# Seven half-size products for the first feed-forward product of two token blocks

## The chip, the cores and the metric

One core of a Trainium2 chip runs the kernel. The metric is the device time of one execution in microseconds (us); lower is better. Each kernel is run several times and the median is given.

## What is computed

A sparse attention over 8 batches, 8 heads and 576 positions is followed by a feed-forward layer over its 4608 x 512 output:

```python
attn = softmax(where(mask, scale * q @ k.T, -1e9))      # heads 0-3: last 32 positions
x = (attn @ v).transpose(0, 2, 1, 3).reshape(4608, 512) # heads 4-7: every 32nd position
h = x @ w_in                                            # 512 x 2048
r = maximum(h, 0)
g = s * (r * r) + b
out = g @ w_out                                         # 2048 x 512
```

The change concerns only `h`, `r` and their squares, for the last 1024 of the 4608 tokens.

## The kernel before

The 4608 tokens are cut into 9 blocks (T = 0 to 8) of 512 tokens. The transposed attention output lies in four tiles `xT` (128 of the 512 features each) that hold three batches of 576 tokens at a time. For each block there is a first product (`ff1`, line 912): for each of 16 groups of 128 hidden features (`ft`), four matmuls of 128 x 128 weights by 512 tokens add up in one bank of PSUM (line 922, 64 matmuls a block). ScalarE takes the bank out with a relu into `u` (line 948), VectorE in a few places (line 950). Two groups at a time are squared into `gT`, on VectorE (line 958) or ScalarE (line 956).

The second product of blocks 0 and 1 is a plain one (`ff2`, line 970). From block 2 on it is `ff2_seven` (line 792): the 512 tokens and 512 output columns are halved, and a Strassen scheme of seven products takes the place of eight quarter products. It needs sums of quarters of `gT` (`sums_post`, line 743, VectorE, line 759), sums of `w_out` formed once (`mix_post`, line 773), 112 matmuls of 256 columns a block (line 890), and evictions that add an earlier result (lines 809, 821 and 832, VectorE). The output goes out by DMA from SyncE's queue.

The order of all instructions comes from a planner (`class Plan`, line 16) that runs while the program is built. It keeps a modelled time, with a cost for each step. TensorE's steps are emitted one by one into a single queue: attention steps, first-product steps and second-product steps. A first-product step goes when what it needs is modelled as done; at every fourth step the second product goes first if the first is more than one block ahead (the main loop at the end of the kernel). Work for the other engines is posted with its needs and a cost for each engine that may take it (`post`, line 41, and `flush`, line 44), and the engine that would be done first gets it. `LATER` lets squares and sums (`g`, `S`) stand back by 1.5 us. PSUM has eight banks in groups `t` (1), `s` (2), `a` (1), `f1` (2) and `f2` (2); a `Group` of matmuls takes the bank of its list that comes free first. On the chip each engine works its queue in order and waits at semaphores.

The last attention steps are issued at about 216 us. After that TensorE has only the two products.

Of the kernel before, what the change touches and what calls it, by code (L numbers as in the profile page):

```python
# [8 lines left out]

FP16 = mybir.dt.float16  # L10
FP32 = mybir.dt.float32
# [4 lines left out]
class Plan:  # L16
# [7 lines left out]
    LAT = {"A": 70.0, "V": 70.0, "P": 70.0, "D": 12000.0, "X": 7000.0, "Y": 12000.0}  # L24

    SLACK = 800.0
    LATER = {"g": 1500.0, "S": 1500.0, "in": 2500.0, "w_mix": 2500.0}

    def __init__(self):
        self.t = 0.0  # L30
# [93 lines left out]
def kernel(  # L124
# [11 lines left out]
    nc = tc.nc  # L136
# [64 lines left out]
    v_str = [const.tile([SQ, 4, ST, D + 1], FP16, name=f"v_str{i}") for i in range(NV)]  # L201
# [16 lines left out]
    p_taken = {True: 0, False: 0}  # L218

    SR = 80  # L220
    ks = [const.tile([SR, 4 * ST * D], FP16, name=f"ks{i}") for i in range(2)]

# [190 lines left out]
    def bank(group):  # L413
        return ps[group.name]
# [310 lines left out]

    SQ_ACT = 0
    SEVEN = 2
    H = NFT // 2

    def ff_order(T):  # L730
        if T < SEVEN:
            return list(range(NFT))
        return [f + g for f in (0, 4) for g in (0, 1, 2, 3, 8, 9, 10, 11)]
# [6 lines left out]
    def roomy(T):  # L740
        return T >= NBLK - 2

    def sums_post(T):

        at2, at4 = ("S2", "S4") if roomy(T) else ((0, 0), (0, 1))
        for h in range(2):
            fs = slice(4 * h, 4 * h + 4)

            def make(out, x, y, op, fs=fs):
                def at(w):  # L750
                    if w in own:
                        if (w, T) not in gts:
                            gts[w, T] = (sp if w == "S" else inp).tile(
                                [128, H, 256], FP16, tag=own[w], name="S")
                        return gts[w, T][:, fs]
                    return part_of(T, *w, fs)

                def g(eng):
                    nc.vector.tensor_tensor(out=at(out), in0=at(x), in1=at(y), op=op)  # L759
# [3 lines left out]
            ns = {"V": 690.0}  # L763
# [28 lines left out]
    def ff2_seven(T):  # L792
# [119 lines left out]
    def ff1(T, ft, ct, group, cts=(0, 1, 2, 3), early=False):  # L912
        tok0 = T * PS
        def f():
            if ft == 0 and ct == cts[0]:
                gts[T] = gp.tile([128, NFT, PS], FP16, tag="gT", name="gT")
            if ct == cts[0]:
                gts["h", T, ft] = bank(group)
            at = tok0 % (NX * S)
            n = min(PS, NX * S - at)  # L920
            for lo, hi in ((0, n), (n, PS))[:1 + (n < PS)]:
                nc.tensor.matmul(  # L922
                    out=gts["h", T, ft][:, lo:hi],
                    lhsT=w_in_sb[ft // 4][:, ct].rearrange("p (x l) -> p l x", l=4)[:, ft % 4],
                    rhs=xT[ct][:, (at + lo) % (NX * S):(at + lo) % (NX * S) + hi - lo],
                    start=(ct == cts[0] and lo == 0), stop=(ct == cts[-1] and hi == PS))

        needs = [("xT", bb, c) for bb in {tok0 // S, (tok0 + PS - 1) // S}
                 for c in ((ct,) if early else range(4))]
        needs.append(("w_in", ft // 4))  # L930
        if ft == 0 and ct == cts[0] and T >= 2:
            needs.append(("F2", T - 2))
        s = Step(f, 216, needs=needs, group=group if ct == cts[0] else None)
        if ft == 0 and ct == cts[0] and T >= SEVEN:
            s.after = lambda: sums_post(T)
        if ct == cts[-1]:
            key = ("h", T, ft)
            s.keys = [key] + ([("F1", T)] if ft == NFT - 1 else [])
# [29 lines left out]
        return s  # L968

    def ff2(T, ts, ft, group, part=0, parts=1):  # L970

# [198 lines left out]
    for T in range(NBLK):  # L1170
        if T == 0:

            gr = [Group("s", SB, "f1", F1B) for _ in range(4)]
            cts = FIRST
            f1 += [ff1(T, ft, ct, gr[ft], cts, True) for ct in cts for ft in range(4)]
        for ft in ff_order(T)[0 if T else 4:]:
            gr = Group("f1", F1B, "f2", F2B) if T == 0 else Group("f1", F1B)
            for ct in range(4):
                f1.append(ff1(T, ft, ct, gr))
        if T == 0:  # L1180

# [12 lines left out]
        if T >= SEVEN:  # L1194
            f2 += ff2_seven(T)
            continue
        for ts in range(4):

            parts = 2 if T == NBLK - 1 and ts == 3 else 1
            for part in range(parts):  # L1200
                gr = Group("f2", F2B)
                for ft in range(NFT):
                    f2.append(ff2(T, ts, ft, gr, part, parts))
                    f2[-1].pos = T + 0.25 + (ts + (part + ft / NFT) / parts) / 4
    plan.t = 1850.0

    def keep_running(until):
# [24 lines left out]

    def due():

        pos = i1 / 64.0 + (f2[i2 - 1].pos if i2 else 0.0) + 0.1
        return (pos if pos <= 1 else 1 + (pos - 1) / 2) * batch_ns

    while i2 < len(f2) or any(at_i[p] < len(att[p]) for p in range(len(att))):
# [14 lines left out]
            order.append(1)  # L1253
        if i2 < len(f2):
            order.append(2)
        if len(order) == 2 and i1 % 4 == 0 and i1 / 64.0 > (f2[i2 - 1].pos if i2 else 0.0) + 1:
            order.reverse()
        if i1 % 4:
            order = [1]
# [53 lines left out]
```

The softmax here doesn't subtract the row's maximum and nothing guards it: scores larger than these inputs give would overflow.

## Time and profile before

| what | value |
|---|---|
| median of 3 runs | 303.96 us (303.76 to 304.38) |
| span of the profiled execution, first to last instruction | 300.1 us |
| difference of the median and that span | 3.86 us |
| TensorE busy | 292.4 us |
| VectorE busy | 220.2 us |
| ScalarE busy | 182.1 us |
| GpSimd busy | 93.0 us |
| granted TensorE clock, mean | 0.998 |

The profiled execution has no separate total: its span runs from its first to its last instruction, and what a run's time has besides is given here as the difference of the median and that span. In a profile, PE is TensorE, PEld its weight loads (which run beside the matmuls), DVE VectorE, ACT ScalarE, POOL GpSimd, SP SyncE. L922 is line 922. The chain of waits is followed back from the last instruction to whatever released it. A row of a group of instructions gives line, engine, operation, output and inputs, shape and count, then busy us and mean ns of one, then the engine's idle time before them and what ended it. Ends of matmuls are modelled, and neighbours overlap, so the distance of their starts says more than their durations.

### The profile page before, as it was taken

What the parts mean: (1) busy time and instruction counts of PE and PEld (TensorE: products, weight loads), DVE (VectorE), ACT (ScalarE), POOL (GpSimd) and SP (SyncE); (2) the same over time, 40 slices, a digit from 0 to 9 for tenths busy, and PEclk for the clock granted to TensorE, in tenths of its full rate; (3) what the DMA queues carried; (4) which work ended last, traced back from release to release, by engine and by line L of the source; (5) the groups of instructions that cost most, each with busy time, mean ns of one, the idle gap of its engine ahead of it and who ended that gap; (6) DMA issues with size and microseconds to landing.
All of it is one profiled execution on the core that took longest, in us unless ns stands there. A gap on an engine that the chain in (4) does not pass through costs nothing.

```text
span 300.1 us, 6846 instructions
## 1 busy us (share of the span) xinstructions
PE 292.4 (97%) x2704; PEld 209.3 (70%) x2704; DVE 220.2 (73%) x462; ACT 182.1 (61%) x326; POOL 93.0 (31%) x140
## 2 busy tenths in 40 slices
PE   7899989999999999999999999999999999999995
PEld 3775655666556558889766876688888577766884
DVE  6857797779876788687877897689766366647663
ACT  3577966889547788638774976488535545444300
POOL 8873442700950495008720494300000000000000
PEclk9999999999999999999999999999999999999999
DMA  8999999999999499999999999996141110200213
GB/s 136 178 204 201 169 214 185 202 163 157 100 189 160 67 128 130 152 181 128 150 137 178 149 170 131 135 154 167 40 96 38 69 35 2 105 0 2 94 66 123
DMA packets 106434, 38.17 MB, mean 127 GB/s; under 512 B 85698, under 2 KB 104258, under 8 KB 106402
## 3 DMA queue, kind: packets, MB, share of 16 engines
q0 software_dynamic: 60848, 18.23, 64.3%
q1 hardware_dynamic: 45554, 19.51, 36.7%
q8 instruction: 21, 0.34, 0.5%
q14 instruction: 11, 0.09, 0.1%
HBM read 36.99 MB, written 10.62 MB: 159 GB/s over the span
## 4 chain that ended last, share of the span: by engine, by line
PE 85%; DMA 9%; POOL 3%; issue 1%; ACT 0%; DVE 0%; POOLq 0%
PE ps_f L922 37%; PE ps_f L890 25%; PE ps_f L979 8%; PE ps_s L565 4%; DMA kl<-in_k_dram 4%; DMA w_out_sb<-in_moe_w_out_dram 3%; PE ps_a L626 2%; DMA vs<-in_v_dram 2%; PE ps_s L890 2%; PE ps_t L626 1%; PE ps_t L890 1%; PE ps_s L979 1%; PE ps_t L444 1%; POOL v_str L346 1%; PE ps_t L673 1%; PE ps_a L890 1%
## 5 line engine op out<-in xcount | busy, mean ns | idle before, releaser
L922 PE MATMUL ps_f<-xT,w_in_sb 128*128 128x512 f16 (+4 forms) x696 | 147.3, 340 | 0.0
L948 ACT ACTIVATE u<-ps_f 128x512 f16<-128x512 f32 x139 | 81.9, 595 | 67.0 <-PE ps_f L922 66.5
L922 PEld LDWEIGHTS <-w_in_sb 128*128 128x128 f16 x704 | 71.7, 113 | 30.6 <-issue 0.3
L890 PEld LDWEIGHTS <-gT 128*128 128x128 f16 x608 | 58.4, 98 | 13.6
L890 PE MATMUL ps_f<-w_out_sb,gT 128*128 128x256 f16 x376 | 53.7, 273 | 0.0
L958 DVE TENSOR_TENSOR gT<-u 128x1024 f16<-128x1024 f16 x48 | 32.8, 684 | 15.0 <-ACT u L948 14.2
L979 PE MATMUL ps_f<-w_out_sb,gT 128*128 128x512 f16 x112 | 29.4, 379 | 0.8 <-DMA w_out_sb<-in_moe_w_out_dram 0.8
L583 ACT ACTIVATE p_str<-ps_s 72x432 f16<-72x432 f32 (+1 forms) x45 | 20.4, 483 | 9.7 <-PE ps_s L565 9.2
L956 ACT ACTIVATE gT<-u 128x1024 f16<-128x1024 f16 x24 | 25.4, 1057 | 0.7
L653 DVE TENSOR_TENSOR x_nat<-ps_a,rec 96x384 f16<-96x384 f32 (+2 forms) x46 | 23.9, 519 | 0.7
L583 ACT ACTIVATE p_loc<-ps_s 128x384 f16<-128x384 f32 x46 | 21.4, 495 | 4.7 <-PE ps_s L565 4.2
L759 DVE TENSOR_TENSOR gT<-gT 128x1024 f16<-128x1024 f16 x34 | 22.5, 682 | 2.1 <-ACT gT L956 1.9
L890 PE MATMUL ps_f<-w_mix,gT 128*128 128x256 f16 x176 | 23.8, 273 | 0.0
L890 PEld LDWEIGHTS <-S 128*128 128x128 f16 x176 | 17.1, 98 | 4.4
L324 POOL DMA_DIRECT2D v_loc<-in_v_dram x24 | 17.8, 766 | 6.9 <-PE ps_f L626 3.8
L979 PEld LDWEIGHTS <-gT 128*128 128x128 f16 x128 | 11.5, 98 | 10.5 <-DMA w_out_sb<-in_moe_w_out_dram 1.2
L329 POOL DMA_DIRECT2D v_str<-in_v_dram x16 | 13.0, 817 | 13.0 <-PE ps_f L890 2.8
L626 PEld LDWEIGHTS <-p_str 72*128 72x128 f16 x256 | 13.2, 98 | 5.4
L1050 POOL COPY gate<-kT 1x1 f16<-1x1 f16 x6 | 2.9, 490 | 45.2 <-DMA kT<-ks 45.1
L643 DVE RECIPROCAL rec<-ps_a 96x6 f32<-96x6 f32 (+2 forms) x46 | 8.4, 183 | 11.3 <-PE ps_a L626 11.1
L890 PE MATMUL ps_f<-w_mix,S 128*128 128x256 f16 x112 | 15.7, 273 | 0.0
L759 DVE TENSOR_TENSOR S<-gT 128x1024 f16<-128x1024 f16 x18 | 11.8, 684 | 0.1
(163 smaller groups left out, 407.3 us busy)
## 6 DMA issues: line engine op xcount, KB each, us to landing
out_dram<-o SPq DMA_DIRECT2D x34, 256.0 KB, 2.4
w_in_sb<-in_moe_w_in_dram POOLq DMA_DIRECT2D x4, 512.0 KB, 10.4
w_out_sb<-in_moe_w_out_dram POOLq DMA_DIRECT2D x4, 512.0 KB, 11.7
qs<-in_q_dram POOLq DMA_DIRECT2D x6, 288.0 KB, 7.3
ks<-in_k_dram POOLq DMA_DIRECT2D x6, 288.0 KB, 9.5
v_loc<-in_v_dram POOLq DMA_DIRECT2D x24, 72.0 KB, 10.0
ql<-in_q_dram POOLq DMA_DIRECT2D x4, 288.0 KB, 9.3
kl<-in_k_dram POOLq DMA_DIRECT2D x16, 72.0 KB, 4.0
```

Of the source, the lines that this page charges most:

```text
L324: nc.gpsimd.dma_start(out=vl[LPAD:128, h, :, 0:D], in_=v_band(b, h))
L329: nc.gpsimd.dma_start(out=vs[:, h, :, 0:D], in_=v[b, 4 + h].rearrange("(p j) d -> p j d", j=ST))
L583: nc.scalar.activation(out=st["pw", g][0:nk, 0:2 * n * nq], in_=st["s", g][0:nk, 0:2 * n * nq], func=AF.Exp, scale=scale)
L626: nc.tensor.matmul(out=st["pa", g][:, n % 6, :], lhsT=st["pw", gp_][0:nk, i * nq:i * nq + WIDE], rhs=vt[0:nk, 2 * mm + e, j, :])
L653: nc.vector.tensor_tensor(out=x_at(0, cnt), in0=st["pa", g][0:nq, 0:cnt, 0:D], in1=st["rec", g][0:nq, 0:cnt].to_broadcast([nq, cnt, D]), o ...
L759: nc.vector.tensor_tensor(out=at(out), in0=at(x), in1=at(y), op=op)
L890: nc.tensor.matmul(out=gts[name, T, t][:, 0] if halves else gts[name, T][:, t], lhsT=lhs(k, t), rhs=rhs(k), start=fresh and k == 0 and (ha ...
L922: nc.tensor.matmul(out=gts["h", T, ft][:, lo:hi], lhsT=w_in_sb[ft // 4][:, ct].rearrange("p (x l) -> p l x", l=4)[:, ft % 4], rhs=xT[ct][: ...
L948: nc.scalar.activation(out=u, in_=gts["h", T, ft], func=AF.Relu)
L956: nc.scalar.activation(out=g, in_=u, func=AF.Square)
L958: nc.vector.tensor_tensor(out=g, in0=u, in1=u, op=ALU.mult)
L979: nc.tensor.matmul(out=gts[id_], lhsT=gts[T][:, ft, ts * 128:(ts + 1) * 128], rhs=w_out_sb[:, ft, cols], start=(ft == 0), stop=(ft == NFT ...
```

## The change

Blocks 7 and 8 (`FIRST7 = NBLK - 2`) no longer go through `ff1`. `ff1_seven` cuts the hidden features (2 x 1024), the input features (2 x 256) and the tokens (2 x 256) in halves and uses the Strassen scheme with seven products. A block has four units of 2 x 256 hidden features; a unit has seven products of four 256-column matmuls each (2 groups of 128 hidden features by 2 of 128 input features), 112 matmuls a block.

- P1, P6, P5 and P3 of a unit add up in one bank, "A". After P1, P6 and P5 its content is copied to an f32 tile (V1, U, E), and the next product waits for that copy. After P3 the bank itself is one quarter of `h`, and a relu takes it out.
- P2 has a bank "C" of its own and is added to V1. P7 has a bank "D" and is added to E; then P4 adds to D, which is added to U.
- The three additions are VectorE's `TENSOR_ADD_SAT`, max(min(a + b, 3e38), 0): the relu is inside the addition. The relu of P3 and the copies may go to ScalarE or VectorE, as may the squares, two per unit.
- `combine_w` forms four sums of quarters of `w_in` on VectorE (eight instructions of 1024 columns) once, after the last attention products. They lie in tiles that the attention had used (`ks`, `v_str`), which grow to 128 partitions.
- `combine_x` forms four differences of quarters of `xT` per block (eight instructions of 256 columns, VectorE), in `qD_loc` for block 7 and `p_loc` for block 8.
- For the last block the second product's order becomes P1, P7, P6, P5, P2, P4, P3 (before, P6 came ahead of P7).
- The main loop's count of first-product steps is 112 for these blocks in place of 64 (`f1_pos`).

```diff
+    FIRST7 = NBLK - 2
+    SUM_P = None
...
-        seq = [seq[i] for i in ((0, 3, 4, 1, 2, 5, 6) if roomy(T) else (0, 2, 3, 4, 1, 5, 6))]
+        seq = [seq[i] for i in ((0, 4, 3, 1, 2, 5, 6) if last else (0, 3, 4, 1, 2, 5, 6) if roomy(T) else (0, 2, 3, 4, 1, 5, 6))]
...
+    def combine_w():
+
+        def w(h, j, i):
+            return w_in_sb[2 * h + i][:, 2 * j:2 * j + 2]
+
+        B1, B2 = B - 2, B - 1
+        AFTER = [("a", (B2, m), 1) for m in range(4)]
...
+        for i in range(2):
+            for n, x, y, op, more in (
+                    (1, w(1, 0, i), w(1, 1, i), ALU.add, []),
+                    (2, w_sum[1][:, i], w(0, 0, i), ALU.subtract, [("wc", 1, i + 1)]),
+                    (3, w(0, 0, i), w(1, 0, i), ALU.subtract, []),
+                    (4, w(0, 1, i), w_sum[2][:, i], ALU.subtract, [("wc", 2, i + 1)])):
+                plan.post(AFTER + held[n] + more, {"V": 690.0},
...
+    def combine_x(T):
...
+            for n, x, y, needs in (
+                    (1, x_part(T, 0, 1, c), x_part(T, 0, 0, c), lo + held),
+                    (3, x_part(T, 1, 1, c), x_part(T, 0, 1, c), lo + hi + held),
+                    (2, x_part(T, 1, 1, c), x_sum(T, 1, c), hi + [("xc", T, 1, c)]),
+                    (4, x_part(T, 1, 0, c), x_sum(T, 2, c), hi + [("xc", T, 2, c)])):
+                plan.post(needs, {"V": 230.0},
...
+    def ff1_seven():
...
+            tags = ("f1", F1B, "t", TB, "a", AB) + (("s", SB) if T < NBLK - 1 else ())
+            A, C, Dd = [Group(*tags) for _ in range(3)]
...
+            def keep(name, pool, tag, st=st, id_=id_):
+                def g(eng):
+                    st[name] = pool.tile([128, PS], FP32, tag=tag, name=name,
+                                         **({"bufs": 3} if tag == "pp" else {}))
+                    copy_on(eng, out=st[name], in_=st["A"])
+                return g
...
+            def add(row, j, of, name, st=st, u_at=u_at):
+                def g(eng):
+                    nc.vector._custom_dve(
+                        TENSOR_ADD_SAT, out=u_at(row, j),
+                        in0=st[of].rearrange("p (t x) -> p t x", t=2),
+                        in1=st[name].rearrange("p (t x) -> p t x", t=2), s0=3.0e38, s1=0.0)
+                return g
...
+            COPY = {"A": 600.0, "V": 690.0}
+            ADD = {"V": 750.0}
+            SQR = {"V": 700.0, "A": 1055.0}
...
+                "P1": ("A", A, True, w_of(0, 0), x_of(0, 0), xn(0, 0), [],
+                       [([key("p1")] + was("c11"), COPY, keep("V1", inp, "ql"), [key("fv")])]),
+                "P2": ("C", C, True, w_of(0, 1), x_of(1, 0), xn(1, 0), [],
+                       [([key("p2"), key("fv")] + free, ADD, add(0, 0, "C", "V1"),
+                         [key("c11"), C])]),
+                "P6": ("A", A, False, s_of(2), t_of(2), tn(2), wn(2) + [key("fv")],
+                       [([key("p6")] + was("c21"), COPY, keep("U", inp, "kl"), [key("fu")])]),
+                "P7": ("D", Dd, True, s_of(3), t_of(3), tn(3), wn(3),
+                       [([key("p7"), key("fe")] + free, ADD, add(1, 1, "D", "E"),
+                         [key("c22")])]),
+                "P5": ("A", A, False, s_of(1), t_of(1), tn(1), wn(1) + [key("fu")],
+                       [([key("p5")] + was("c22"), COPY, keep("E", inp, "pp"), [key("fe")])]),
+                "P4": ("D", Dd, False, w_of(1, 1), t_of(4), tn(4), [key("c22")],
+                       [([key("p4"), key("fu")] + free, ADD, add(1, 0, "D", "U"),
+                         [key("c21"), Dd]),
+                        ([key("c21"), key("c22"), ("F2", T - 2)], SQR, square(1),
+                         [("g", T, ft + 8), ("g", T, ft + 9)])]),
+                "P3": ("A", A, False, s_of(4), x_of(1, 1), xn(1, 1), wn(4) + [key("fe")],
+                       [([key("p3")] + free, COPY, relu, [key("c12"), A]),
+                        ([key("c11"), key("c12"), ("F2", T - 2)], SQR, square(0),
+                         [("g", T, ft), ("g", T, ft + 1)])]),
...
+        for i in range(len(units) + 1):
+            for back, name in ((0, "P1"), (1, "P3"), (0, "P2"), (0, "P6"), (0, "P7"), (1, "P4"),
+                               (0, "P5")):
+                if 0 <= i - back < len(units):
+                    order += steps[units[i - back] + (name,)]
...
-        for ft in ff_order(T)[0 if T else 4:]:
+        for ft in ff_order(T)[0 if T else 4:] if T < FIRST7 else ():
...
+        if T == FIRST7:
+            f1 += ff1_seven()
...
+    cut = 64 * FIRST7
+    f1_pos = [i / 64.0 if i < cut else FIRST7 + (i - cut) / 112.0 for i in range(len(f1) + 1)]
```

In the order of the units, a unit's P3 and P4 come among the next unit's products: P1, the last unit's P3, P2, P6, P7, the last unit's P4, P5. Block 7 may use six banks for A, C and D (`f1`, `t`, `a`, `s`), block 8 four (without `s`).

More of the change, by code (lines that the diff above doesn't have):

```diff
@@ L8 @@
 from concourse._compat import with_exitstack
+from concourse.dve_ops import TENSOR_ADD_SAT
 FP16 = mybir.dt.float16
@@ L26 @@
     SLACK = 800.0
-    LATER = {"g": 1500.0, "S": 1500.0, "in": 2500.0, "w_mix": 2500.0}
+    LATER = {"g": 1500.0, "S": 1500.0, "in": 2500.0, "w_mix": 2500.0, "wc": 1500.0}
     def __init__(self):
@@ L200 @@
     v_loc = [const.tile([128, 4, LT, D + 1], FP16, name=f"v_loc{i}") for i in range(NV)]
-    v_str = [const.tile([SQ, 4, ST, D + 1], FP16, name=f"v_str{i}") for i in range(NV)]
+    v_str_home = [const.tile([128, 4, ST, D + 1], FP16, name=f"v_str{i}") for i in range(NV)]
+    v_str = [x[0:SQ] for x in v_str_home]
     kT_loc = [const.tile([128, LPAD + S], FP16, name=f"kT_loc{i}") for i in range(2)]
@@ L220 @@
     SR = 80
-    ks = [const.tile([SR, 4 * ST * D], FP16, name=f"ks{i}") for i in range(2)]
+    ks_home = [const.tile([128, 4 * ST * D], FP16, name=f"ks{i}") for i in range(2)]
+    ks = [x[0:SR] for x in ks_home]
     QB_DMA, KB_DMA, QS_DMA, XS_DMA = 5, 4, 3, 4
@@ L758, in g @@
                 def g(eng):
-                    nc.vector.tensor_tensor(out=at(out), in0=at(x), in1=at(y), op=op)
+                    {"V": nc.vector, "P": nc.gpsimd}[eng].tensor_tensor(
+                        out=at(out), in0=at(x), in1=at(y), op=op)
                 return g
@@ L762, in sums_post @@
             gh = [("g", T, f + H) for f in range(4 * h, 4 * h + 4)]
-            ns = {"V": 690.0}
+            ns = {"V": 690.0, **({"P": SUM_P} if T >= FIRST7 and SUM_P else {})}
             free = [("P7", T - 1)] if T > SEVEN else []
@@ L968, in ff1, with x_sum @@
         return s
+    homes = {1: ks_home[0], 2: ks_home[1],
+             3: v_str_home[0].rearrange("p h t d -> p (h t d)")[:, 0:2048],
+             4: v_str_home[1].rearrange("p h t d -> p (h t d)")[:, 0:2048]}
+    w_sum = {n: x.rearrange("p (i c f) -> p i c f", i=2, c=2) for n, x in homes.items()}
+    def x_sum(T, n, c):
+        tl = (qD_loc if T % 2 else p_bufs[True])[(n - 1) // 2]
+        flat = tl.rearrange("p t e c -> p (t e c)") if T % 2 else tl
+        at = 512 * ((n - 1) % 2) + 256 * c
+        return flat[:, at:at + 256]
@@ new lines, in x_part, with on @@
+    def x_part(T, k, j, c):
+        at = T * PS % (NX * S) + 256 * j
+        return xT[2 * k + c][:, at:at + 256]
+    def on(eng):
+        return {"V": nc.vector, "P": nc.gpsimd}[eng].tensor_tensor
+    def combine_w():
[3 more added lines that the diff above has]
+        AFTER = [("a", (B2, m), 1) for m in range(4)]
+        held = {1: [("k", (B1, m)) for m in (2, 3)], 2: [("k", (B2, m)) for m in (2, 3)],
+                3: [("a", (B1, m), 2) for m in (2, 3)], 4: [("a", (B2, m), 2) for m in (2, 3)]}
+        for i in range(2):
[5 more added lines that the diff above has]
+                plan.post(AFTER + held[n] + more, {"V": 690.0},
+                          lambda eng, n=n, x=x, y=y, op=op, i=i: on(eng)(
+                              out=w_sum[n][:, i], in0=x, in1=y, op=op), [("wc", n, i + 1)])
@@ new lines, in combine_x @@
+    def combine_x(T):
+        tok0 = T * PS
+        bs = {tok0 // S, (tok0 + PS - 1) // S}
+        held = [("s", (B - 1, m), 2) for m in range(2)] if T % 2 else [
+            ("a", (B - 1, m), 1) for m in range(2)]
+        for c in range(2):
+            lo, hi = [("xT", b, c) for b in bs], [("xT", b, c + 2) for b in bs]
+            for n, x, y, needs in (
[4 more added lines that the diff above has]
+                plan.post(needs, {"V": 230.0},
+                          lambda eng, n=n, x=x, y=y, c=c: on(eng)(
+                              out=x_sum(T, n, c), in0=x, in1=y, op=ALU.subtract),
+                          [("xc", T, n, c)])
@@ new lines, in ff1_seven, with w_of, s_of, x_of @@
+    def ff1_seven():
+        units = [(T, u) for T in range(FIRST7, NBLK) for u in range(4)]
+        steps = {}
+        for at, (T, u) in enumerate(units):
+            ft = (0, 2, 4, 6)[u]
+            tags = ("f1", F1B, "t", TB, "a", AB) + (("s", SB) if T < NBLK - 1 else ())
+            A, C, Dd = [Group(*tags) for _ in range(3)]
+            id_ = (T, u)
+            st = {}
+            old = units[at - 2] if at >= 2 else None
+            def w_of(h, j, ft=ft):
+                return lambda t, c: w_in_sb[2 * h + ft // 4][:, 2 * j + c].rearrange(
+                    "p (x l) -> p l x", l=4)[:, (ft + t) % 4]
+            def s_of(n, ft=ft):
+                return lambda t, c: w_sum[n][:, ft // 4, c].rearrange(
+                    "p (x l) -> p l x", l=4)[:, (ft + t) % 4]
+            def x_of(k, j, T=T):
+                return lambda c: x_part(T, k, j, c)
+            def t_of(n, T=T):
+                return lambda c: x_sum(T, n, c)
+            def keep(name, pool, tag, st=st, id_=id_):
[4 more added lines that the diff above has]
+                return g
+            def u_at(row, j, st=st, ft=ft):
+                if ("u", row) not in st:
+                    st["u", row] = (xnp if row else up).tile(
+                        [128, 2, PS], FP16, tag="xs" if row else "u", name="u")
+                return st["u", row][:, :, 256 * j:256 * j + 256]
+            def add(row, j, of, name, st=st, u_at=u_at):
[5 more added lines that the diff above has]
+                return g
+            def relu(eng, st=st, u_at=u_at):
+                if eng == "A":
+                    nc.scalar.activation(out=u_at(0, 1), in_=st["A"].rearrange(
+                        "p (t x) -> p t x", t=2), func=AF.Relu)
+                else:
+                    nc.vector.tensor_relu(out=u_at(0, 1), in_=st["A"].rearrange(
+                        "p (t x) -> p t x", t=2))
+            def square(row, st=st, T=T, ft=ft):
+                def g(eng):
+                    if T not in gts:
+                        gts[T] = gp.tile([128, NFT, PS], FP16, tag="gT", name="gT")
+                    x = st["u", row]
+                    g_ = gts[T][:, ft + 8 * row:ft + 8 * row + 2, :]
+                    if eng == "A":
+                        nc.scalar.activation(out=g_, in_=x, func=AF.Square)
+                    else:
+                        nc.vector.tensor_tensor(out=g_, in0=x, in1=x, op=ALU.mult)
+                return g
+            def key(x, id_=id_):
+                return (x,) + id_
+            def was(x, old=old):
+                return [(x,) + old] if old else []
+            far = ff_order(T - 1)[8 + 4 * u:12 + 4 * u] if u < 2 else [
+                x + y for x in (ft - 4, ft + 4) for y in (0, 1)]
+            free = [("g", T - 1 if u < 2 else T, x) for x in far]
+            COPY = {"A": 600.0, "V": 690.0}
+            ADD = {"V": 750.0}
+            SQR = {"V": 700.0, "A": 1055.0}
+            bs = [T * PS // S]
+            both_b = sorted({T * PS // S, (T * PS + PS - 1) // S})
+            def xn(k, j, bs=bs, both_b=both_b):
+                return lambda c: [("xT", b, 2 * k + c) for b in (both_b if j else bs)]
+            def tn(n, T=T):
+                return lambda c: [("xc", T, n, c)]
+            def wn(n, ft=ft):
+                return [("wc", n, ft // 4 + 1)]
+            prods = {
+                "P1": ("A", A, True, w_of(0, 0), x_of(0, 0), xn(0, 0), [],
[19 more added lines that the diff above has]
+                         [("g", T, ft), ("g", T, ft + 1)])]),
+            }
+            for name, (bk, group, fresh, lhs, rhs, needs, more, posts) in prods.items():
+                steps[T, u, name] = mine = []
+                for t in range(2):
+                    for c in range(2):
+                        def f(t=t, c=c, bk=bk, group=group, fresh=fresh, lhs=lhs, rhs=rhs, st=st):
+                            if fresh and t == c == 0:
+                                st[bk] = bank(group)
+                            nc.tensor.matmul(
+                                out=st[bk][:, 256 * t:256 * t + 256], lhsT=lhs(t, c), rhs=rhs(c),
+                                start=fresh and t == c == 0, stop=t == c == 1,
+                                skip_group_check=True)
+                        mine.append(Step(f, 110, needs=needs(c) + more,
+                                         group=group if fresh and t == c == 0 else None))
+                mine[-1].keys = [key(name.lower())]
+                if name == "P3" and u == 3:
+                    mine[-1].keys = mine[-1].keys + [("F1", T)]
+                mine[-1].posts = posts
+            if u == 0:
+                first = steps[T, u, "P1"][0]
+                first.after = lambda T=T: sums_post(T)
+        order = []
+        for i in range(len(units) + 1):
[3 more added lines that the diff above has]
+                    order += steps[units[i - back] + (name,)]
+        return order
@@ L1204 @@
                     f2[-1].pos = T + 0.25 + (ts + (part + ft / NFT) / parts) / 4
+    combine_w()
+    for T in range(FIRST7, NBLK):
+        combine_x(T)
     plan.t = 1850.0
@@ L1233, in due @@
     def due():
-        pos = i1 / 64.0 + (f2[i2 - 1].pos if i2 else 0.0) + 0.1
+        pos = f1_pos[i1] + (f2[i2 - 1].pos if i2 else 0.0) + 0.1
         return (pos if pos <= 1 else 1 + (pos - 1) / 2) * batch_ns
@@ L1255 @@
             order.append(2)
-        if len(order) == 2 and i1 % 4 == 0 and i1 / 64.0 > (f2[i2 - 1].pos if i2 else 0.0) + 1:
+        if len(order) == 2 and i1 % 4 == 0 and f1_pos[i1] > (f2[i2 - 1].pos if i2 else 0.0) + 1:
             order.reverse()
```

## The prediction

> **What bounds the kernel now.** I read the page's busy table first, then the groups of the last stage by tile shape, then the chain of waits, then the busy time by stage.
>
> ```profile
> PE 292.4 (97%) x2704; PEld 209.3 (70%) x2704; DVE 220.2 (73%) x462; ACT 182.1 (61%) x326; POOL 93.0 (31%) x140
> PEclk9999999999999999999999999999999999999999
> PE 85%; DMA 9%; POOL 3%; issue 1%; ACT 0%; DVE 0%; POOLq 0%
> ```
>
> TensorE (PE) is busy for 97% of the span and carries 85% of the chain that ended last; the granted clock is full. That is an average, so the stage of the change has to be looked at by itself. Its chain of waits, in order of time (start, us, what):
>
> ```profile
> 222.67 0.87 PE ps_f L922 x8
> 223.54 0.76 PE ps_f L890 x7
> ...
> 252.01 0.86 PE ps_f L922 x4
> 252.87 0.76 PE ps_f L890 x7
> 253.63 0.86 PE ps_f L922 x4
> 254.50 4.04 PE ps_f L890 x37
> ...
> 284.36 1.75 PE ps_t L890 x16
> ...
> 295.71 0.89 PE ps_f L890 x8
> 296.60 0.02 issue
> 296.62 0.48 DVE o L821
> ```
>
> Each piece ends where the next begins: from 232.5 to 296.6 us nothing but TensorE stands in the chain. L922 is the first product (a 512-column matmul costs 0.86/4 = 0.216 us), L890 the second, already seven products of 256 columns (1.75/16 = 0.109 us). The sum over the stage, 128 x 0.216 + 336 x 0.109 = 64.3 us, against 64.1 us of chain, says the same: TensorE's instruction stream is the time. What the other engines do there, by stage:
>
> ```profile
> core 0: us, PE busy (x) PEld busy (x) DVE busy (x) ACT busy (x) POOL busy (x), PEclk, DMA share, GB/s
> 210.00:232.50 22.50, 22.50 (x227) 18.98 (x225) 15.02 (x31) 10.58 (x17) 0.00 (x0) 1.00 0.24 57
> 232.50:258.50 26.00, 26.00 (x177) 18.17 (x176) 15.97 (x25) 12.55 (x19) 0.00 (x0) 1.00 0.12 41
> 258.50:280.50 22.00, 22.00 (x142) 14.53 (x140) 12.15 (x18) 9.96 (x16) 0.00 (x0) 1.00 0.11 37
> 280.50:297.10 16.60, 16.08 (x148) 14.17 (x145) 10.43 (x16) 1.65 (x2) 0.00 (x0) 1.00 0.26 91
> ```
>
> The second row is first product of block 7 beside second product of block 6, the third is blocks 8 and 7, the fourth is what is left of the second products. VectorE (DVE) and ScalarE (ACT) have 38% to 55% free in the two rows that the change touches.
>
> **What is removed on TensorE.** Two blocks times 16 x 4 matmuls of 512 columns: 128 x 0.216 = 27.65 us, all on the path. **What is added there:** two blocks x 4 units x 7 products x 4 matmuls of 256 columns = 224. At the 0.109 us of L890 that is 24.45 us, so 3.2 us less. This needs weight loads at twice the rate, and the loads of this product are the slower kind:
>
> ```profile
> L922 PEld LDWEIGHTS <-w_in_sb 128*128 128x128 f16 x64 | 7.2, 113 | 4.3
> L890 PEld LDWEIGHTS <-gT 128*128 128x128 f16 x96 | 9.4, 98 | 2.9
> ```
>
> The new weights keep the same stride of four columns, so 113 ns, and not 98, is the load to reckon with. If such loads followed one another at 113 ns, the 224 would cost 25.3 us and the gain would be 2.3. The trace has a near row: block 6's first product wraps round the end of xT, so its matmuls are split (384 and 128 columns) with the same strided loads, and the chain has eight of them in 0.87 us (222.67 above): 0.109 us per load. I take 0.109.
>
> A rule speaks against the change here. The Trainium skill, "TensorE: Matmul & The Clock Gate", Part 3, The mechanism, lists that a weight load overlaps a running matmul only if the row group differs (the same section also lets the background weight buffer be filled ahead). All loads here use all rows. By the first sentence every pair would be load plus matmul: 113 + 216 = 329 ns before, 113 + 109 = 222 ns after, 49.7 us for the 224 instead of 42.1 us for the 128, a loss of 7.6 us. The row at 222.67 has a load for each matmul and 0.109 us for the pair, so the loads lie under the matmuls; the measurement decides.
>
> **What is added on VectorE and ScalarE.** Per block before: 16 relus on ACT (0.597 us) and 8 squares (DVE 0.69 or ACT 1.057). After: 12 copies of an accumulator and 4 relus, at 0.57 (the f32 copy of the b sums, ACT) to 0.60 on ACT: 16 x 0.6 = 9.6 us, as before; the 8 squares stay. New on DVE are 12 additions with relu of a PSUM and an f32 SBUF operand. The trace has no such operation: below, a plain f32 addition (L832) at 0.69; above, addition and relu (L950, 0.69) one after the other, 1.38. Nearest is the eviction L821, two operations in one pass on the same kinds of operands, 0.75, which I take: 9.0 us. The differences of x are 8 per block of 256 f16 columns: from 0.684 us for 1024 columns and 0.745 for 1152, 0.48 ns a column, so an estimate of 0.3 us each, 2.5 us. VectorE's fixed part per block is then 9.0 + 2.5 + sums of g 8 x 0.684 = 5.5 + seven evictions 5.3 + the addition Ub 0.7 = 23.0 us in a stage that shrinks to about 24.4 (112 x 0.109 for either product). That is 94% full before any square, so the planner has to give the squares to ACT: 9.6 + 8 x 1.057 = 18.1 us of 24.4. It fits, but with little room on VectorE. Durations of neighbours overlap a little (two sums take 1.28, not 1.37), so true filling is nearer 88%.
>
> The sums of w_in, 8 x 0.684 = 5.5 us, are asked for once the last attention batch is done (about 214 us) and the first half by block 7's third product (about 235 us). The first row shows 7.5 us of DVE idle, and 3.4 us of squares there can move to ACT, which idles 11.9 us. Cover is there; without it, block 7 would start up to 1 us behind, and second-product matmuls of block 6 would run first. I take nothing.
>
> **New waits.** A first-product bank used to be written once and evicted. Now one bank carries P1, P6, P5 and P3 in turn, each waiting until the last content is copied out. With four matmuls of each product in turn a product comes every 0.87 us. P1 to P6 and P6 to P5 have two other products between, 1.7 us and more, against 0.04 (matmul end to ACT start in the timeline) + 0.6 + about 0.1 = 0.75. P5 to P3 is the tight one: one product and its partner group, 1.3 us, slack 0.5. Behind a waiting matmul stands all of TensorE's queue, second product included. If ACT has just begun a square (1.06), the copy is up to 0.5 late: at 35% of ACT's time in squares, 0.35 x 0.56 x 0.56 / (2 x 1.06) = 0.05 us per unit, 0.4 over eight units. For additions behind a full VectorE queue (P4 waits for P7's, second product's P2, P3, P4 for evictions) I add 0.3. Bounds: nothing (the stage has no gap now; less than nothing is excluded, since TensorE's own work is a floor) and 4 us (0.5 in each of eight units). I take 0.7, near the low end, because an order is planned with these waits known and the other product fills them.
>
> **The end.** At the end of block 8's first product, the last unit's P5, P3, P4 follow each other: copy 0.75, P7's addition 0.85, then P4, 1.6 us with only second product to run. About 28 matmuls of block 7's second product are left over (the rule lets the first lead by that much), some 3 us; before, 32 matmuls (280.86 to 284.36) lay there. Then P1 of block 8 (1.75) runs while the last square and sums finish; P7 before P6 gives the sum S2 another 1.75. The last product and its store are unchanged. No cost taken; 0 to 1 us.
>
> **Sum.** 300.1 - 3.2 + 0.7 = 297.6 us of span. The span is one execution's; the median of the runs is 303.96, 3.86 above it, which I carry over: 301.5 us. With the estimate 301.5 the floor is 303.96 - 3.2 = 300.8, give or take 0.2.
>
> **The rivals.**
> 1. TensorE still sets the pace, with small gaps: 300.6 to 302.5, likeliest 301.5. For it: the gapless chain, the known spacing. Chance 0.62.
> 2. Hand-offs eat most of it: VectorE at nine tenths is late with evictions, so both products wait at once, or the last block, with four banks in place of six, finds none free. 0.25 us in each of eight units plus 0.5 at the end: 303.96 - 3.2 + 2.5 = 303.3 (302.5 to 304.8). For it: ACT and DVE fully committed; against it: the two products can fill each other's waits. Chance 0.28, a little over half of it below 303.35.
> 3. Slower: the fused addition with relu costs like two operations and VectorE sets the pace of both blocks. Its work per block is 14.0 + 12a; it passes the shrunk stage (24.4) at a = 0.87 and the old one (26.0) at a = 1.0. At a = 1.38 it is 30.6, 4.6 over the old stage, twice: 303.96 + 9.2 = 313. Against it: L821 does two operations in 0.75. Chance 0.07, with any other slower end.
> 4. It doesn't do what it says: the strided loads can't be fed at 0.109 when no 384-column matmul stands between, 113 ns or more: at 123 ns the 224 cost the old 27.6 us and nothing is won: 304.0 + 0.3. Chance 0.03.
>
> **Chances and range.** About 0.2% (0.6 us) is what a measurement of this kernel can tell from no change: below 303.35 is faster. Case 1 and 0.15 of case 2: 0.77; within: 0.13 (0.10 of case 2, and case 4); slower 0.10 (case 3, and 0.03 of case 2). Range 300.6 to 303.8: case 1, most of 2, leaving out 3.
>
> **What would show it.** The 256-column matmuls of the first product at 0.109 us apart (0.113 or more: step one wrong); TensorE's busy share still whole between 232 and 280 (gaps, and their releaser, price the new waits: ACT copy for P3, DVE for P4 or the evictions); the fused addition near 0.75; squares mostly on ACT; VectorE near 90% busy in those stages; the last matmul about 2.5 us earlier than 296.6. A VectorE without idle time and an addition over 1 us would make the prediction wrong.

## The result

The changed kernel takes 300.86 us in the median of 8 runs (300.25 to 302.57), the kernel before 303.38 in the median of 8 (302.43 to 304.38). The ratio on record is 0.9933, 95% interval 0.9911 to 0.9956: about 2.0 us faster. The two medians alone would say 2.5 us, but three of the eight runs before are those of the table ahead of the prediction (303.76 to 304.38), and the other five lie at 302.43 to 303.59 with a median of 302.91. Against these the ratio of medians is 0.9932. A second set of runs gave 300.82 against 303.02, ratio 0.9932 (0.9906 to 0.9958). The forecast was 301.5, with a range of 300.6 to 303.8.

The spans of the two profiled executions differ by only 1.3 us, so the page of the changed kernel has to be read with care:

```profile
span 298.8 us, 7101 instructions
...
PE 289.0 (97%) x2800; PEld 219.2 (73%) x2800; DVE 236.6 (79%) x500; ACT 191.9 (64%) x335; POOL 94.1 (32%) x141
...
PE 84%; DMA 10%; POOL 3%; ACT 1%; issue 1%; DVE 0%; POOLq 0%; ACTq 0%
```

TensorE is 3.4 us less busy, VectorE 16 us busier, and TensorE is still the chain. About as much again as the difference of the spans was lost far ahead of the change, where TensorE's first matmul on w_out waits for that load. Here is that place in the chain of waits, before and then after (start, us, what):

```profile
29.83 9.44 DMA w_out_sb<-in_moe_w_out_dram
...
39.32 0.61 PE ps_f L979 x2
```

```profile
30.81 9.80 DMA w_out_sb<-in_moe_w_out_dram
...
40.66 0.61 PE ps_f L1183 x2
```

The load landed 1.34 us later in the second execution. TensorE hardly idles afterwards (up to the change, two gaps of under 0.1 us in either trace), so it carries that to the end. From that matmul on, the rest takes 298.8 - 40.66 = 258.1 us against 300.1 - 39.32 = 260.8: 2.6 us less. So the comparison below uses the last stage alone: from the end of the last attention matmul (line 626 before, 629 after) to the end of the last matmul in the chain. These are the lines of the chain, the last attention matmuls before and after, and the last matmuls after (those of before, at 295.71, stand in the prediction):

```profile
215.45 0.12 PE ps_t L626 x4
...
215.91 0.12 PE ps_t L629 x4
...
294.32 0.89 PE ps_f L896 x8
```

The planner's order leaves some of block 6's first product over at the start of this stage. These are the matmuls of the old first product in it, L922 before and L928 after (stretch, its length, PE busy, PEld busy, PEclk, DMA share, GB/s):

```profile
215.57:296.60 81.03, 40.11 (x192) 20.27 (x192) 1.00 0.16 52
216.04:295.20 79.16, 9.17 (x72) 6.36 (x70) 1.00 0.16 54
```

Before, 128 of the 192 belong to blocks 7 and 8. The other 64, and the 72 after, are halves of block 6's split groups of 512 columns: 32 groups before, 36 after. A group takes 2 x 0.109 = 0.218 us, and this is taken off for each of the four more. Before, the stage is 81.03 us. After, it is 79.16 - 4 x 0.218 = 78.29: **2.74 us shorter**.

The busy time by stage, after (the same stretches as before; the work lies up to 1.4 us later in the first and up to 1.4 us earlier in the last):

```profile
core 0: us, PE busy (x) PEld busy (x) DVE busy (x) ACT busy (x) POOL busy (x), PEclk, DMA share, GB/s
210.00:232.50 22.50, 22.50 (x232) 19.06 (x230) 20.20 (x48) 16.75 (x23) 1.59 (x1) 1.00 0.20 56
232.50:258.50 26.00, 25.72 (x237) 24.22 (x235) 21.77 (x37) 14.67 (x21) 0.00 (x0) 1.00 0.12 43
258.50:280.50 22.00, 22.00 (x204) 20.81 (x202) 18.56 (x30) 13.38 (x19) 0.00 (x0) 1.00 0.11 38
```

VectorE went from 61% and 55% to 84% in the two rows of the change, and TensorE is whole but for 0.28 us in one of them. The chain shows that place, and below it stands VectorE's queue there:

```profile
239.73 0.44 PE ps_f L896 x4
240.17 0.45 PE ps_t L1153 x4
240.62 0.03 ACTq L349
240.64 0.04 issue
240.69 0.59 ACT E L349
241.28 0.04 issue
241.32 0.60 PE ps_t L1153 x4
```

```profile
239.77 0.69 DVE L1073 CUSTOM_DVE_ANT_0 u<-ps_a,U 128x512 f16<-128x512 f32 x1 [1.71 <-PE ps_a L1153]
240.38 0.74 DVE L815 SCALAR_TENSOR_TENSOR Va<-ps_f,s_sb,bcs 128x512 f32<-128x512 f32 x1
```

L1153 is the seven-product form. Its four matmuls of 256 columns take 0.44 us, 0.109 each, as forecast. At 240.62 a P5 ends, the copy of its bank (E) runs on ScalarE, and the same unit's P3 waits for it. One more product (the next unit's P1, 0.44 us) runs meanwhile. The second product could not fill the rest: its P1 (block 6) had ended at 240.17, and its P2 needs the eviction Va, which VectorE ran from 240.38 to 241.12, right after a fused addition. So the planner's order has three products of the first kind in a row there. The four matmuls of P3 then take 0.60 and not 0.44, since three of their four weight loads came only after the wait as well. The whole loss is 0.27 + 0.16 = 0.43 us.

New or moved operations on VectorE and ScalarE, grouped by shape, from 210 us on:

```profile
L1073 DVE CUSTOM_DVE_ANT_0 u<-ps_f,U 128x512 f16<-128x512 f32 x4 | 2.8, 690 | 0.7 <-PE ps_f L1153 0.7
...
L1028 DVE TENSOR_TENSOR p_loc<-xT,p_loc 128x256 f16<-128x256 f16 x4 | 1.1, 284 | 0.0
...
L1094 ACT ACTIVATE gT<-u 128x1024 f16<-128x1024 f16 x13 | 13.8, 1059 | 1.7 <-DVE u L1073 1.4
...
L1096 DVE TENSOR_TENSOR gT<-u 128x1024 f16<-128x1024 f16 x3 | 2.1, 689 | 0.1
```

The fused addition (L1073) takes 0.69 us, as long as one plain operation on such a tile; 13 of the 16 squares went to ScalarE.

### The profile page after: what moved, and what is told of

Read it like the earlier page. It is cut to its first block, busy times and chain, and to the rows that moved or that the text cites. A ratio compares the mean times of both kernels' runs of the same rounds, so it can differ in the third digit from the quotient of the medians.

```text
span 298.8 us, 7101 instructions
## 1 busy us (share of the span) xinstructions
PE 289.0 (97%) x2800; PEld 219.2 (73%) x2800; DVE 236.6 (79%) x500; ACT 191.9 (64%) x335; POOL 94.1 (32%) x141
## 4 chain that ended last, share of the span: by engine, by line
PE 84%; DMA 10%; POOL 3%; ACT 1%; issue 1%; DVE 0%; POOLq 0%; ACTq 0%
PE ps_f L928 28%; PE ps_f L896 25%; PE ps_f L1183 8%; DMA kl<-in_k_dram 4%; PE ps_s L568 4%; DMA w_out_sb<-in_moe_w_out_dram 3%; PE ps_f L1153 3%; PE ps_a L629 2%; DMA vs<-in_v_dram 2%; PE ps_t L1153 2%; PE ps_a L1153 2%; PE ps_s L896 2%; PE ps_s L1153 2%; PE ps_t L629 1%; PE ps_t L896 1%; PE ps_s L1183 1%
## 5 line engine op out<-in xcount | busy, mean ns | idle before, releaser
L928 PE MATMUL ps_f<-xT,w_in_sb 128*128 128x512 f16 (+4 forms) x568 | 115.5, 331 | 0.0
L954 ACT ACTIVATE u<-ps_f 128x512 f16<-128x512 f32 x107 | 62.8, 594 | 34.2 <-PE ps_f L928 32.6
L928 PEld LDWEIGHTS <-w_in_sb 128*128 128x128 f16 x576 | 57.4, 114 | 22.7 <-DMA w_in_sb<-in_moe_w_in_dram 0.8
L896 PEld LDWEIGHTS <-gT 128*128 128x128 f16 x608 | 58.5, 98 | 9.6
L896 PE MATMUL ps_f<-w_out_sb,gT 128*128 128x256 f16 x376 | 54.9, 273 | 0.0
L962 ACT ACTIVATE gT<-u 128x1024 f16<-128x1024 f16 x24 | 25.4, 1058 | 0.7
L964 DVE TENSOR_TENSOR gT<-u 128x1024 f16<-128x1024 f16 x32 | 21.8, 682 | 4.5 <-ACT u L954 4.0
L896 PE MATMUL ps_f<-w_mix,gT 128*128 128x256 f16 x176 | 24.9, 273 | 0.0
L896 PEld LDWEIGHTS <-S 128*128 128x128 f16 x176 | 17.1, 98 | 3.0
L896 PE MATMUL ps_f<-w_mix,S 128*128 128x256 f16 x112 | 15.7, 273 | 0.0
L1094 ACT ACTIVATE gT<-u 128x1024 f16<-128x1024 f16 x13 | 13.8, 1059 | 1.7 <-DVE u L1073 1.4
```

The costliest lines, as they stand in the source:

```text
L896: nc.tensor.matmul(out=gts[name, T, t][:, 0] if halves else gts[name, T][:, t], lhsT=lhs(k, t), rhs=rhs(k), start=fresh and k == 0 and (ha ...
L928: nc.tensor.matmul(out=gts["h", T, ft][:, lo:hi], lhsT=w_in_sb[ft // 4][:, ct].rearrange("p (x l) -> p l x", l=4)[:, ft % 4], rhs=xT[ct][: ...
```

## The experiments

The theory: TensorE's columns set the last stage, weight loads and VectorE's new work lie beside them, and the one loss is the gap at 241 us. Rivals: the loads cost something of their own; the sums, the hand-offs, the banks or VectorE's queue eat part of the gain; the last block's new order makes part of it. "Stage" is the length defined above (81.03 before, 78.29 changed).

**Loads alone.** The kernel before, with the first product of blocks 7 and 8 in half-size matmuls, eight products as ever:

```diff
-            for lo, hi in ((0, n), (n, PS))[:1 + (n < PS)]:
+            parts = ((0, n), (n, PS))[:1 + (n < PS)]
+            if T >= NBLK - 2:
+                parts = ((0, 256), (256, PS))
+            for lo, hi in parts:
```

> The kernel before, with every first-product matmul of the last two blocks cut into two halves of 256 columns: same products, twice the weight loads (256 in place of 128). Theory (loads lie under the matmuls, 0.109 us a pair): 256 x 0.109 = 27.9 against 27.65 us, within 0.3 us of before (303.4). Rival (strided loads follow one another at 113 ns): +1.3 us. Rival (loads don't overlap matmuls of the same rows): the pair costs 222 ns, 56.8 us in place of 27.65, some 29 us slower.

303.31 us against 303.08, ratio 1.0006 (0.9989 to 1.0024); stage 81.35, 0.32 longer. In its chain eight half-size matmuls with the strided loads take 0.87 us:

```profile
263.48 0.87 PE ps_f L925 x8
264.35 0.33 PE ps_f L890 x3
```

128 more loads, with their matmuls, cost those 0.3 us, while each load is recorded at 113 ns beside matmuls 109 ns apart. The serial rule that the prediction weighed (29 us here) and the 113 ns spacing (1.3 us) both fall.

**The sums alone.** `ff1_seven` is left out and `ff1` serves all blocks, but `combine_w` and `combine_x` run; nothing reads what they form. The last block's old order and the old count of first-product steps are put back with it (not shown here).

```diff
-        for ft in ff_order(T)[0 if T else 4:] if T < FIRST7 else ():
+        for ft in ff_order(T)[0 if T else 4:]:
...
-        if T == FIRST7:
-            f1 += ff1_seven()
```

> Only the sums of w_in and the differences of x are added (24 VectorE instructions, 5.5 + about 4.5 us by their durations); both blocks keep the eight-product form and nothing reads the sums. Theory (TensorE sets the time, VectorE has idle time to hide them): within 0.3 us of before. Rival (VectorE's queue delays evictions): up to 1 us slower, with TensorE gaps released by DVE in the stage from 210 to 235 us.

303.25 against 303.08, ratio 0.9995 (0.998 to 1.001); four groups more are left over at the start of its stage, 81.90 - 4 x 0.218 = 81.03, the same as before. The 24 instructions are hidden whole, and TensorE has no gap, though VectorE is busy for 20.3 of 22.5 us between 210 and 232.5.

**One block.** `FIRST7 = NBLK - 1`.

> Seven products for the last block alone. Theory (columns of TensorE): half of 3.2 us, with no gap if the copy of E stays hidden in the last block: 1.6 us faster than before, 301.8. Rival (a fixed cost at the end or from the sums): less than 1.0 us faster. Rival (the gain is mostly the last block's new order): the full 2.5 us.

301.57 against 303.08, ratio 0.9952 (0.9935 to 0.9968). Five extra groups were left over at the start of its stage: 80.53 - 5 x 0.218 = 79.44, 1.59 us shorter, with no gap. That is half of 3.2, as the columns say.

**The last block's order undone.**

```diff
-        seq = [seq[i] for i in ((0, 4, 3, 1, 2, 5, 6) if last else (0, 3, 4, 1, 2, 5, 6) if roomy(T) else (0, 2, 3, 4, 1, 5, 6))]
+        seq = [seq[i] for i in ((0, 3, 4, 1, 2, 5, 6) if roomy(T) else (0, 2, 3, 4, 1, 5, 6))]
```

> The changed kernel with the old order of the last block's second product (P6 ahead of P7). In the changed kernel's trace the sum S2 that P6 needs is done at 284.35 us and P1 ends at 284.71. Theory: P6 could have started there, so no change (within 0.2 us). Rival (the new order is part of the gain): 0.5 to 1 us slower, with a TensorE gap at about 284.7 us released by DVE S.

300.37 against 303.07, ratio 0.9906 (0.9892 to 0.9919); stage 78.29, the changed kernel's own. The order gives nothing, the sum S2 being ready anyway. With the same stage, the ratio came out 0.003 from the changed kernel's 0.9933: so much can come from the draw of runs, and stages are the finer measure.

**More room for the copy of E.** P2 goes ahead of the last unit's P3, so two products stand between P5 and P3.

```diff
-            for back, name in ((0, "P1"), (1, "P3"), (0, "P2"), (0, "P6"), (0, "P7"), (1, "P4"),
+            for back, name in ((0, "P1"), (0, "P2"), (1, "P3"), (0, "P6"), (0, "P7"), (1, "P4"),
```

> The changed kernel with the order P1, P2, P3 of the unit before, P6, ...: two products and not one between P5 and P3 of a unit. Theory (the only loss in the new stage is the wait of P3 for the copy E, 0.43 us with the weight loads it holds back): no TensorE gap after 216 us, 0.4 us faster than the changed kernel, 0.8% or more below before. Rival (banks or VectorE give other waits when C is taken earlier): the gap goes elsewhere, no gain.

300.06 against 303.08, ratio 0.9898 (0.9879 to 0.9916). The gap is gone, though at the same place the second product still stood back for three groups:

```profile
239.66 0.44 PE ps_f L896 x4
240.10 0.44 PE ps_t L1153 x4
240.54 0.44 PE ps_s L1153 x4
240.97 0.44 PE ps_f L1153 x4
241.41 0.44 PE ps_t L1153 x4
241.85 1.75 PE ps_f L896 x16
```

The stage is 77.86: 3.17 below before, the whole of the 3.2 us that the columns give, and 0.43 below the changed kernel, the whole of the gap's price. VectorE is as full in this version (84% and 85% of the two rows). A second set on one chip with the changed kernel:

> The changed kernel once more, to see how much of a difference of two versions is the draw of runs. Theory (the last stage is 2.7 us shorter, everything ahead of it is the same): a ratio near 0.991, inside or at the lower end of the first interval. Rival (0.9933 is the size of it): 0.993 or more.

> The order P1, P2, P3 of the unit before once more, beside the changed kernel on the same chip. Theory: 0.4 us below the changed kernel, ratio near 0.990. Rival: no difference of the two that goes beyond their intervals.

The changed kernel 300.82, ratio 0.9932 (0.9906 to 0.9958); this order 299.87, ratio 0.990 (0.9877 to 0.9923), both against 303.02. Stages 78.30 and 77.87. The rival for the first has the ratio right (0.993), while its stage says 0.991; between sets of 4 to 8 runs the head of the kernel, with its loads, moves by as much. The intervals of the two versions overlap, so that this order is better is shown by the stages of both pairs of traces and by the medians' direction twice, not by a clear interval.

**Less room.** A unit's P3 comes right after its P5.

```diff
-            for back, name in ((0, "P1"), (1, "P3"), (0, "P2"), (0, "P6"), (0, "P7"), (1, "P4"),
+            for back, name in ((1, "P3"), (0, "P1"), (0, "P2"), (0, "P6"), (0, "P7"), (1, "P4"),
```

> The changed kernel with P3 of a unit right after its P5: the copy of E (0.59 us and about 0.15 of hand-off) has to fit under second-product matmuls alone. Theory (the two products fill each other's waits because the order is planned): at most 0.3 us a unit, within 0.6 us of the changed kernel. Rival (hand-offs stall TensorE): 0.3 to 0.75 us in each of eight units, 2.4 to 6 us slower than the changed kernel, gaps released by ACT E.

300.44 against 303.07, ratio 0.9905 (0.989 to 0.992); stage 78.58, 0.29 longer than the changed kernel. In seven of eight units the tight hand-off costs nothing. The only gap is again where block 6's P2 waits for Va behind a fused addition:

```profile
239.28 0.47 DVE u L1073
...
239.89 0.75 DVE Va L815
...
240.68 1.14 PE ps_f L896 x9
```

The copy of E was late there too: it ran on ScalarE only from 240.97 to 241.54, behind a square that had begun at 240.00. The nine matmuls of the second product filled the end of that wait. In both gaps, this one and the changed kernel's, the two products waited at once. In no other unit did TensorE wait for a copy.

**Banks.** The version with P2 ahead of P3 with four banks for block 7 too, then the changed kernel with three in both blocks:

```diff
-            tags = ("f1", F1B, "t", TB, "a", AB) + (("s", SB) if T < NBLK - 1 else ())
+            tags = ("f1", F1B, "t", TB, "a", AB)
```

```diff
-            tags = ("f1", F1B, "t", TB, "a", AB) + (("s", SB) if T < NBLK - 1 else ())
+            tags = ("f1", F1B, "t", TB)
```

> The version r2_late with four banks in place of six for block 7 too. Theory (a unit holds A for about 8.2, C for 1.4 and D for 8.3 us of its 6.1: under three banks on the mean, four at most): no change, within 0.2 us of r2_late. Rival (banks limit the product): 0.5 us or more slower, with TensorE gaps between 230 and 256 us.

> The changed kernel in its own order with three banks (f1 and t) for A, C and D in both blocks. Theory: 2.9 banks are wanted on the mean and three are there, so each product waits for a release, the second product runs ahead and is used up, then TensorE idles: 2 us or more slower than the changed kernel. Rival (the second product still fills it all): within 0.5 us.

Four banks: 300.34 against 303.02, ratio 0.9908 (0.989 to 0.9927), stage 77.86, no gap. Three banks: 300.67, ratio 0.9926 (0.9904 to 0.9948), stage 78.44, 0.15 longer than the changed kernel. My expectation of 2 us for three banks was wrong: the second product filled nearly all that the banks held up, in longer and less regular stretches (L896 in pieces of up to 14 in place of 4). The changed kernel's wait for E is not in this trace. In its place stand two others, 0.3 us each, behind Va at 241 us and behind a fused addition at 264.5.

**VectorE's room.** Each fused addition twice (the second repeats the first into the same place), with the planner told:

```diff
-                    nc.vector._custom_dve(
+                    for _ in range(2):
+                        nc.vector._custom_dve(
...
-            ADD = {"V": 750.0}
+            ADD = {"V": 1360.0}
```

> The changed kernel with each fused addition issued twice (24 more on VectorE, told to the planner as 1.36 us): VectorE's work per block goes from about 18.9 us of queue (12 x 0.60 + 8 x 0.20 + 8 x 0.60 + 7 x 0.67 + 0.6, without squares) to 26.1, past the stage's 24.45. Theory (VectorE's room was real but small): 1.5 to 4 us slower than the changed kernel, so about as slow as before or slower. Rival (VectorE is far from setting the pace): within 0.5 us of the changed kernel.

303.17 against 303.07, ratio 1.0 (0.9991 to 1.001): the gain is gone. Stage 81.39, 3.10 longer than the changed kernel. VectorE is 95% and 98% busy in the two rows (columns as above):

```profile
232.50:258.50 26.00, 25.72 (x237) 24.26 (x235) 24.64 (x41) 15.48 (x23) 1.27 (x1) 1.00 0.11 40
258.50:280.50 22.00, 20.43 (x185) 18.75 (x183) 21.65 (x35) 13.45 (x19) 1.59 (x1) 1.00 0.08 28
```

The first row, at 95%, has only the changed kernel's own gap of 0.28 us. The loss comes later. By the distance of the matmuls' starts it is 2.1 us between 265 and 271 us and 1.0 us at 285.5, and the longest of TensorE's waits (waiting, what for, us, times, longest) are these:

```profile
PE ps_t L896 <- DVE u L1074: 0.8, 1, 0.8
PE ps_a L1154 <- ACT u L1082: 0.7, 1, 0.7
PE ps_f L1154 <- DVE u L1074: 0.7, 1, 0.7
```

**Squares on VectorE alone.**

```diff
-            SQR = {"V": 700.0, "A": 1055.0}
+            SQR = {"V": 700.0}
```

> The changed kernel with the squares of the last two blocks allowed on VectorE alone (13 of 16 had gone to ScalarE): VectorE's queue per block goes to 18.9 + 4.8 = 23.7 us of 24.45. Theory: nearly full, so gaps of TensorE of 0.3 to 1.5 us in sum. Rival (squares anywhere are hidden): within 0.2 us. Rival (ScalarE was what held the copies back): faster by the gap of 0.4 us.

302.49 against 303.07, ratio 0.9977 (0.9961 to 0.9992); stage 80.37, 2.08 longer than the changed kernel, more than the 0.3 to 1.5 expected. TensorE's waits after 213 us (waiting, what for, us, times, longest):

```profile
PE ps_f L896 <- DVE S L764: 1.0, 1, 1.0
PE ps_f L1153 <- DVE u L1073: 0.6, 1, 0.6
PE ps_t L1153 <- ACT E L349: 0.3, 1, 0.3
```

VectorE is busy 22.97 of 26 and 19.85 of 22 us in the two rows, 88% and 90%, against 84% in the changed kernel. But the 2.08 us are not spread over the rows. The first has only the known gap; the second, by the distance of the matmuls' starts, loses 0.90 us between 267 and 272 us; and 1.17 us lie behind both rows, at 287 us. There the last square ends on VectorE at 285.33 us. VectorE then stands idle for 0.40 us until it can start the eviction Va, and only behind that comes the sum that TensorE waits for:

```profile
285.73 0.75 DVE Va L815
286.48 0.61 DVE S L764
...
287.13 3.23 PE ps_f L896 x28
```

So more than half of the price is the order of VectorE's last operations, and not how full it is in the two rows.

## Why the prediction held, point by point

- **TensorE's columns, -3.2 us: right.** The order with P2 ahead of P3 shows 3.17 without any gap, one block alone 1.59.
- **Spacing of the strided loads at 0.109 us: right.** Half-size matmuls in the old form cost 0.32 us for 128 more loads. The row of the split block 6 was the near one, and the rule of the Trainium skill ("TensorE: Matmul & The Clock Gate", Part 3, The mechanism), that loads overlap only across row groups, does not hold here: loads of all rows lie under running matmuls. The background weight buffer, which the same section allows for, would explain it; no run here shows whether it does.
- **Sums and differences at nothing: right** (the stage is the same to 0.01 us). Estimated 0.3 us for a difference of x, measured 0.28.
- **The fused addition at 0.75: measured 0.69,** the lower bound. With it VectorE is 84% full in the two rows, where the prediction reckoned with about 88%. At twice its cost it would have taken the gain away; doubled, it did, though the rival's 313 us were far too high. That sum took recorded durations, which overlap: in the queue the next instruction starts 0.61 us after a fused addition (239.77 to 240.38 above). With such distances the expectation's sum for the doubled run is 26.1 us a block in a stage of 24.45, 1.65 over, twice: 3.3 us, and 3.10 was measured.
- **New waits, 0.7 us: mis-sized, 0.43.** The mechanism as argued (a square ahead of the copy of E, a little in each of eight units) is not what was seen. There was one gap, with ScalarE idle when the copy was wanted; what was missing was the other product, held by an eviction on VectorE. That both products wait at once is the mechanism of rival 2, for one unit of eight. The argument that the other product fills such waits was right, as the tight order shows. A square ahead of the copy does occur in that run, and there, too, it cost only together with the wait for Va.
- **Banks: no limit.** Four are as good as six (stage 77.86 either way); three cost 0.15 us against the changed kernel.
- **The end: nothing, right,** but not for P7's place in the order, which gives nothing.
- **3.86 us around the span: wrong.** Runs whose spans are known, of either kernel, lie 1.7 to 1.9 us above them (300.66 to 298.8 in the profiled one). So the profiled execution of before took about 301.9 us by this difference (an estimate), less than any of the eight runs. Its w_out load landed at 39.3 us, earlier than in any other chain here in which that load stands. Because the predicted time was the median less 2.5, this did no harm.
- **The starting point, 303.96, was 0.6 to 1 us high** (medians of later and larger sets: 303.02 to 303.08). This is why the measured 300.86 lies at the prediction's floor of 300.8. The gain itself was forecast as 2.5 us; the ratio says 2.0 and the stage 2.74.
- **The last matmul 2.5 us earlier: seen as 1.4** (296.60 to 295.21), for the w_out load that landed 1.34 later.

The stage is what the change does. The 0.7 us by which the ratio falls short of it, in two sets of runs, lie outside the stage. That they are only the draw of runs is likely but not shown: the version with the old order of the last block has the same stage and came out at 0.9906, while w_out landed at 39.3 us in the one trace of before, at 40.35 in that of the split run, whose program is the same up to block 7, and at 40.6 and 40.7 in the two traces of the changed kernel.

## What to carry to other kernels

When one engine is the chain without a gap, count its columns: half-size products that keep the matmul rate gave all of that count (3.17 of 3.2 us), and everything else was worth knowing only for where it makes that engine wait. With two independent streams in one queue, a late hand-off costs nothing as long as the other stream is ready, so look for the moments at which both wait, and give room there; here one swap of two products was worth 0.43 us. The share of busy time of an engine beside the chain does not give the price by itself: with VectorE at 84% the loss was 0.43 us in one order and nothing in another, a row at 95% lost no more than that order's own gap, and the two versions that filled VectorE further lost their 2 to 3 us in a few waits, a third of it in one and over half in the other at the end of the last block. So look for the single waits, and for what the fuller engine still has to do when the last product needs it.

## What the runs showed of the hardware

A sum of f16 tiles on VectorE stretched from 0.68 to 1.77 us while GpSimd ran an f32 addition of 1.59 us. VectorE and then GpSimd in the changed kernel (start, us, engine):

```profile
221.13 1.28 DVE L764 TENSOR_TENSOR gT<-gT 128x1024 f16<-128x1024 f16 x2
222.33 0.74 DVE L815 SCALAR_TENSOR_TENSOR Ua<-ps_f,s_sb,Va 128x512 f32<-128x512 f32 x1
223.00 2.37 DVE L1011 TENSOR_TENSOR v_str<-w_in_sb,ks 128x1024 f16<-128x1024 f16 x2
```

```profile
223.22 1.59 POOL L838 TENSOR_TENSOR Ub<-Ua,bcs 128x512 f32<-128x512 f32 x1 [29.70 <-DVE Ua L815]
```

Two sums that take 1.28 us elsewhere took 2.37: the first 0.68, the second, which began at 223.59 beside the addition, 1.77. It is the same in all eleven traces here in which GpSimd does this addition at this place (1766 to 1776 ns for the second sum). In the run with one block of seven products VectorE does the addition itself, and the same two sums take 0.68 us each:

```profile
221.05 0.68 DVE L1011 TENSOR_TENSOR v_str<-w_in_sb,ks 128x1024 f16<-128x1024 f16 x1
...
222.31 0.68 DVE L1011 TENSOR_TENSOR v_str<-w_in_sb,ks 128x1024 f16<-128x1024 f16 x1
222.91 0.68 DVE L838 TENSOR_TENSOR Ub<-Ua,bcs 128x512 f32<-128x512 f32 x1
```

Not every instruction is stretched. In the run with squares on VectorE alone, a square (f16, read from SBUF) that began 0.37 us into such an addition of 1.27 us took 1.45 us in place of 0.68. In the run with doubled additions, fused additions, with one operand in PSUM, ran beside GpSimd's in their usual 0.68 and 0.69, and so did a sum that had begun before it. So the stretching goes with GpSimd's addition, and only for some instructions; what the two engines share is not shown.

The addition had been done by VectorE in 0.69 us before and was handed to GpSimd because VectorE was modelled as busy: it cost VectorE 1.09 us to be spared 0.69. Here it was hidden.
